# A fused spectral filter and gated MLP on one core: contiguous blocks for the channel products, a held load queue and one zero product less

## The chip, the cores and the metric

The kernel runs on one core of one Trainium2 chip. The metric is the device time of one execution in microseconds. The kernel before was timed three times: 181.11 us is the median, and the runs lie between 180.49 and 181.13 us. One more execution was recorded by the profiler. It took 181.27 us, of which 179.5 us are the span from the first to the last instruction of the program, and every instruction time below comes from it.

## The reference

```python
def reference(A_x, A_w_r, A_w_i, B_x, B_w_gate, B_w_up, B_w_down):
    ...
    x = A_x                                    # (1, 2048, 512) bf16
    xn = _layernorm(x, axis=-1)
    return x + _A_ref(xn, A_w_r, A_w_i) + _B_ref(xn, B_w_gate, B_w_up, B_w_down)
```

`_A_ref` is a two-dimensional real FFT over 2048 tokens and 512 channels, a product with the complex weight `w_r + i w_i` (2048 x 257), and the inverse FFT. `_B_ref` is a gated MLP: `(gelu(xn @ w_gate) * (xn @ w_up)) @ w_down` with an inner width of 1792. Both see the same normalised `xn`, and `B_x` is not used.

## The kernel before, in words

**Stages.** The 2048 tokens are 16 blocks of 128 (`s`), in four groups of four blocks (`b`). For each block VectorE takes the statistics (`stats`, L496 and L497) and normalises (`norm`, L513); TensorE transposes by a product with an identity matrix (`turn`, L526), and VectorE copies the result to `xnT` (L531). The MLP works on `xnT`: `first` (L669) makes the first three of 14 chunks of the inner width for the first two blocks alone, in products of 128 columns, `gated` (L650) all others, in products of 256 and then 512 columns, with gelu and copy on ScalarE (L655, L656) and the product of both on VectorE (L657); `down` (L695) multiplies by `w_down`.

**The spectral half.** For each group `fold` (L537) adds and subtracts mirrored channels on VectorE and then makes two *channel products* (`f_c`, L555 to L566): eight matmuls each, L563, into two PSUM banks of a tile `ps_sp`, from the folded tokens `z` and the small cosine and sine tables `Tf`. Four of the eight have 128 columns (frequencies 0 and 2 modulo 4), four have 256 (odd frequencies). ScalarE then copies the 1024 columns of the tile into `Y` (L569), with the frequencies in order. Token transforms (L776), the weight product on VectorE, inverse token transforms (L851, L852) and inverse channel products (L916) follow.

In PSUM a bank of 512 columns is seen as `(s r i)`: two halves `s` (cosine, sine), two rows `r` (even, odd), 128 columns `i`. The 128-column products share the even row: one writes its columns 0, 2, 4, ..., the other 1, 3, 5, .... The 256-column products write the odd rows as two runs of 128 neighbours:

```python
bank = spb(t, o).rearrange("p (s r i) -> p s r i", s=2, r=2)
even = bank[:, :, 0].rearrange("p s (i h) -> p s i h", h=2)
...
    to = even[:, :, :, cc] if cc < 2 else bank[:, :, 1]
    mat = Tf.ap[:, cc] if cc < 2 else Tf.ap[:, 2 * cc - 2:2 * cc]
    ins = e.matmul(to, z.ap[:, j, o, cc * P:(cc + 1) * P], mat, start=(cc == 0), stop=(cc == 3))
```

**Order of the work.** Every operation is noted with an engine, an estimated cost and a key. A planner (`_Sched.run`, L184) then goes through a model of the five engines and one DMA pipe and fixes for each engine the order in which it issues; `emit` (L249) writes that order out with semaphore waits. TensorE takes up spectral work as soon as the model has it ready, and MLP products, in a fixed order (`fkey`), otherwise. The planner's cost of a channel product is `4 * 0.057 + 4 * 0.11`, 0.67 us.

**Loads.** SyncE (SP) issues nearly all DMAs, in this order: four loads of 128 KB with blocks 0 to 3 of `x`; `wg` and `wu` columns 384 to 768; blocks 4 to 7 of `x`; `wg` and `wu` columns 768 to 1280 and 1280 to 1792; the rest of `small` (the tables `Tf`, `Ti`); blocks 8 to 15 of `x`; `wd`, `tokf`, `toki`; the mirrored copies of the spectral weight, and the weight itself. ScalarE's queue issues three loads at the start: the identity (part 0 of `small`, 32 KB), and columns 0 to 384 of `wg` and `wu` (384 KB each). No load waits for anything but its own data.

**The start.** Before data arrives TensorE runs products on a tile of zeros (`warm`, L483, 128x512): ten with key -50 (`WARM`), and two more with key -30 that the planner puts right behind them. Then come the transposes of block 0, `first` on block 0, the transposes of block 1 and so on.

Of the kernel before, what the change touches and what calls it, by code (L numbers as in the profile page):

```python
# [7 lines left out]
ACT = mybir.ActivationFunctionType  # L8
# [7 lines left out]
P = 128  # L16
NFC = 14
NHALF = 6
NFIRST = 3
WARM = 10  # L20
HKEY = 1.5
NORM = 14.0, 1.5
STAT = 13.0, 1.6
# [12 lines left out]
def _constants():  # L36
    npbf = mybir.dt.np(BF16)
    th = 2.0 * np.pi / S
    m = np.arange(P)
    K = np.zeros((8, P))  # L40
    K[0] = 8 * (2 * (m % 64) + m // 64)
    for v, c in enumerate((4, 1, 9, 2, 10, 3, 11)):
        K[v + 1] = c + 16 * m
    q = np.arange(P) + 0.5
    ph = th * q[:, None, None] * K[None]
    co, si = np.cos(ph), np.sin(ph)
    si2 = si.copy()
    si2[:, 0, 0] = np.sin(th * q * 1024)
    cof = co.copy()
    cof[:, 0, 0] *= 0.5  # L50
    tf = np.stack([cof, si2, -si2], 1)
    ci, sv = co[:64].transpose(2, 1, 0), si2[:64].transpose(2, 1, 0)
    sg = np.array([0, 1, 1, 1, 1, -1, -1, -1])[:, None]
    pr = np.concatenate([ci, -sg * sv], 2)
    pi = np.concatenate([sv, sg * ci], 2)
    lo = (m < 64)[:, None]
    for a in (pr, pi):
        half = a[:, 0, 0:64].copy()
        a[:, 0] = np.concatenate([half * lo, half * ~lo], 1)
    ti = np.stack([pr, pi, -pi], 2)  # L60
    a = 2.0 * np.pi / D * (np.arange(P) + 0.5)[:, None]
    ke = 2 * np.arange(P)[None]
    kse = ke.copy()
    kse[0, 0] = 256
    T = np.stack([np.cos(a * ke), np.cos(a * (ke + 1)), np.sin(a * kse), np.sin(a * (ke + 1))], 1)
    al = np.full((P, 4), 2.0)
    al[0, 0] = al[0, 2] = 1.0
    Ti = T.transpose(2, 1, 0) * al[:, :, None] / (S * D)
    fwd = []
    for d0, r, n in ((0, 0, 64), (0, 2, 64), (0, 1, P), (P, 1, P)):  # L70
        kk = np.arange(r, 256, 4 if n == 64 else 2)[None]
        ks = np.where(kk == 0, 256, kk)
        a = 2.0 * np.pi / D * (d0 + np.arange(P) + 0.5)[:, None]
        fwd += [np.cos(a * kk), np.sin(a * ks)]
    small = np.concatenate([np.eye(P)] + fwd + [Ti.reshape(P, 512)], 1)

    def cvt(z):
        return np.ascontiguousarray(z.reshape(P, -1).astype(np.float32).astype(npbf))

    return cvt(small), cvt(tf), cvt(ti)  # L80
# [47 lines left out]
class _Sched:  # L128
# [11 lines left out]
    def op(self, eng, cost, fn, reads=(), writes=(), tiles=(), key=0.0, after=(), dma=0, lag=0.0, due=None):  # L140
        o = _Op()
        o.eng, o.fn, o.cost, o.key, o.dma, o.lag, o.due = eng, fn, cost, key, dma, lag, due
        o.reads, o.writes, o.tiles = reads, writes, [(t, False) for t in tiles]
        o.extra = [a for a in after if a is not None]
        o.seq = len(self.ops)
        o.end = None
        o.pos = None
        self.ops.append(o)
        return o
# [182 lines left out]
def bass_parallel_sum__spectral_gfnet__glu_gated_geglu__prompt_kernel(  # L332
# [11 lines left out]
    c_small = nc.inline_tensor(small_np, name="c_small")  # L344
# [9 lines left out]
    sch = _Sched()  # L354
    op = sch.op

    with ExitStack() as es:
        def sb(name, shape, dt=BF16, cell=0):
            n = int(np.prod(shape))
            t = es.enter_context(nc.sbuf_tensor(name, [P, n], dt))  # L360
            return view(t, name, 0, shape, cell)
# [18 lines left out]
        small = sb("smallc", [11, P])  # L380
# [22 lines left out]
        ident = small[:, 0]  # L403
# [18 lines left out]
        def spb(t, h, lo=0, n=512):  # L422
            b = (2 * t.slot + h) * 512 + lo
            return ps_sp[:, b:b + n]

        def spair(t):
            return ps_sp[:, t.slot * 1024:(t.slot + 1) * 1024]
# [10 lines left out]
        def c_act(n):  # L438
            return 0.17 + n * 0.000833

        def dma(q, dst, src, nbytes, wr=None, rd=None, key=0.0, after=(), cost=0.41, lag=0.0):
            return op(q, cost, lambda e: e.dma_start(dst() if callable(dst) else dst.ap, src() if callable(src) else src.ap),  # L442
                      reads=rd if rd is not None else (), writes=wr if wr is not None else (), dma=nbytes, key=key, after=after, lag=lag)

        def tt(o, a, b, f, n, key=0.0, **kw):
            return op("dve", c_tt(n), lambda e: e.tensor_tensor(o.ap, a.ap, b.ap, f), reads=(a, b), writes=(o,), key=key, **kw)  # L446
# [4 lines left out]
        def load(q, dst, src, nbytes, **kw):  # L451
            return dma(q, dst, lambda: src, nbytes, wr=(dst,), **kw)

        def blk(s):
            return (s - 1) % 16

        def wload(q, dst, src, lo, hi, **kw):
            load(q, dst[:, :, lo:hi], src[:, :, lo:hi], (hi - lo) * 1024, **kw)

        k = iter(np.arange(0.0, 1.0, 0.001))  # L460
        for s in range(4):
            load("sp", x[:, s], xb[:, blk(s), :], 131072, key=next(k))
        load("act", ident, c_small.ap()[:, 0:P], 32768, key=-9)
        wload("act", wg, wgv, 0, 384, key=0.5)
        wload("act", wu, wuv, 0, 384, key=0.5)
        for w, v in ((wg, wgv), (wu, wuv)):
# [2 lines left out]
        for lo, hi in ((768, 1280), (1280, FF)):  # L469
            for w, v in ((wg, wgv), (wu, wuv)):  # L470
                wload("sp", w, v, lo, hi, key=next(k))
        load("sp", small[:, 1:11].rs([10 * P]), c_small.ap()[:, P:], 327680, key=next(k))
        for b in (2, 3):
            load("sp", x[:, 4 * b:4 * b + 4], xb[:, 4 * b - 1:4 * b + 3, :], 524288, key=next(k))
        op("pool", 0.1, lambda e: e.memset(eps.ap, LN_EPS), writes=(eps,), key=-2)
# [6 lines left out]
        def warm(key):  # L482
            op("pe", 0.38, lambda e: e.matmul(ps_dn[:, :], zero.ap[:, 0:P], zero.ap, start=True, stop=True), reads=(zero,), tiles=(wt,), key=key)  # L483

        for _ in range(WARM):
            warm(-50)


        def xs(s):
            return x[:, s]  # L490
# [4 lines left out]
        def stats(s, key, due=None, after=()):  # L495
            op("dve", 0.63, lambda e: e.bn_stats(bst[:, s].ap, xs(s).ap), reads=(xs(s),), writes=(bst[:, s],), key=key, due=due, after=after)  # L496
            op("dve", 0.172, lambda e: e.bn_aggr(bag[:, s].ap, bst[:, s].ap), reads=(bst[:, s],), writes=(bag[:, s],), key=key, due=due)  # L497
# [36 lines left out]
        Y = R1(0, [8, 2, D])  # L534
        H = R3(0, [8, 2, D])
        X = R1(0, [8, 2, D])
        def fold(b):  # L537
            par = b % 2
            a = RB(2048 * par, [4, 2, P])
            f = RB(4096 + 2048 * par, [4, 4, P])  # L540
            z = R3(2048 * par, [2, 2, 512])
            xt = xnT[:, b]
            kk = 2.0
            tt(a, xt[:, :, 0:2], xt[:, :, 2:4], ADD, 1024, kk)
            tt(f[:, :, 0], a[:, :, 0], a[:, :, 1], ADD, 512, kk)
            tt(f[:, :, 1], a[:, :, 0], a[:, :, 1], SUB, 512, kk)
            tt(f[:, :, 2:4], xt[:, :, 0:2], xt[:, :, 2:4], SUB, 1024, kk)
            fv = f.rs([2, 2, 4, P])
            zv = z.rs([2, 2, 4, P])
            tt(zv[:, :, 0], fv[:, :, 1], fv[:, :, 0, :, ::-1], ADD, 1024, kk)  # L550
            tt(zv[:, :, 1], fv[:, :, 1], fv[:, :, 0, :, ::-1], SUB, 1024, kk)
            for j in range(2):
                t = _T("sp")

                def f_c(e, z=z, j=j, t=t):  # L555
                    ins = None
                    for o in range(2):
                        bank = spb(t, o).rearrange("p (s r i) -> p s r i", s=2, r=2)
                        even = bank[:, :, 0].rearrange("p s (i h) -> p s i h", h=2)
                        for cc in range(4):  # L560
                            to = even[:, :, :, cc] if cc < 2 else bank[:, :, 1]
                            mat = Tf.ap[:, cc] if cc < 2 else Tf.ap[:, 2 * cc - 2:2 * cc]
                            ins = e.matmul(to, z.ap[:, j, o, cc * P:(cc + 1) * P], mat, start=(cc == 0), stop=(cc == 3))  # L563
                    return ins

                op("pe", 4 * 0.057 + 4 * 0.11, f_c, reads=(z[:, j], Tf), tiles=(t,), key=kk, lag=0.1)  # L566
                jp = 2 * b + j
                yv = Y[:, jp].rs([4, P, 2])
                op("act", c_act(1024), lambda e, yv=yv, t=t: e.activation(yv.ap, spair(t).rearrange("p (s r i) -> p s i r", s=4, r=2), ACT.Copy),  # L569
                   writes=(yv,), tiles=(t,), key=-0.5)  # L570

        stats(0, -60.0)
        stats(1, -55.0, None, (sch.ops[-1],))
        root_act(0, 1, -60.0)
        op("act", 1.5, lambda e: e.activation(tmp.ap, eps.ap, ACT.Gelu_apprx_tanh), reads=(eps, rs[:, 0:1]), writes=(tmp,), key=-30.0)
# [9 lines left out]
        for s in (2, 3):  # L585
            norm(s, -50.0)
            turn(s, 1, -50.0)
        fold(0)
        for s in range(4, 16):
            stats(s, 0.0, STAT[0] + STAT[1] * (s - 4))  # L590
# [170 lines left out]
        for v in range(8):  # L761
            c = v // 2
            t = _T("sp")
# [75 lines left out]
        for v in range(8):  # L839
            t = _T("sp")  # L840
# [61 lines left out]
        for jq in range(4):  # L902
# [6 lines left out]
            for jp in (2 * jq, 2 * jq + 1):  # L909
                t = _T("sp")  # L910
# [57 lines left out]
```

## Time and profile before

| what | value |
|---|---|
| median of three runs | 181.11 us |
| the profiled execution | 181.27 us, span 179.5 us |
| TensorE (PE) busy | 173.8 us, 97% of the span |
| VectorE (DVE) busy | 137.6 us, 77% |
| ScalarE (ACT) busy | 108.0 us, 60% |
| channel products L563 | 64 matmuls, 3.9% of the span in the chain that ended last |
| copies of their tiles L569 | 8, 1022 ns each |
| DMA, first quarter of the span | mostly 330 to 367 GB/s |

Busy times count an engine's instructions, not its waits. The profile ends a matmul by a model, so that two matmuls in a row overlap in it; what a matmul costs TensorE is read from the distance between starts, or from the chain that ended last, which gives each piece the time that it added. A `q` behind an engine's name is its sequencer, which issues DMAs. A load is listed with the time from its issue to its landing.

### The profile page before, as it was taken

The numbers are of one execution on the slowest core, as the hardware profiler recorded it, in microseconds if no ns is written. First come the engines' busy times: TensorE is split into PE (matmuls) and PEld (weight loads), VectorE is DVE, ScalarE is ACT, GpSimd is POOL, SyncE is SP. The second block draws the span as 40 slices with busy tenths as digits, with TensorE's granted clock in tenths as the row PEclk, the third lists the DMA queues.
The fourth block names the chain that finished last, engine by engine and source line by source line (L and its number), as shares of the span: only waits on it lengthen the run. The fifth ranks groups of instructions, "written<-read, shape, count | busy, mean of one in ns | idle before, by whom it ended". The sixth has DMA issues, their size and how long they took to land.

```text
span 179.5 us, 2752 instructions
## 1 busy us (share of the span) xinstructions
PE 173.8 (97%) x1042; PEld 93.2 (52%) x1054; DVE 137.6 (77%) x269; ACT 108.0 (60%) x173; POOL 8.0 (4%) x19
## 2 busy tenths in 40 slices
PE   7699999999999999999999999999999999999994
PEld 2398555645466644444444464464444466544443
DVE  2479699987754799429999949949999935995931
ACT  3368766665385865896655386695746389873000
POOL 3120202300000000000000000000000000000000
PEclk9999999999999999999999999999999999999999
DMA  5999997222563600000000000000000000330311
GB/s 153 330 347 358 349 367 265 59 60 52 108 148 76 174 0 0 4 0 0 0 0 0 4 2 0 0 4 0 0 0 0 5 0 0 102 106 29 117 58 60
DMA packets 17773, 14.97 MB, mean 83 GB/s; under 512 B 1247, under 2 KB 17376, under 8 KB 17760
## 3 DMA queue, kind: packets, MB, share of 16 engines
q1 hardware_dynamic: 16560, 13.98, 26.1%
q10 hardware_dynamic: 1200, 0.82, 1.5%
q8 instruction: 8, 0.13, 0.3%
q14 instruction: 5, 0.04, 0.1%
HBM read 12.70 MB, written 3.15 MB: 88 GB/s over the span
## 4 chain that ended last, share of the span: by engine, by line
PE 94%; DMA 4%; ACTq 1%; issue 0%; DVE 0%
PE ps_gu L650 52%; PE ps_dn L695 20%; PE ps_sp L695 7%; PE ps_sp L563 4%; DMA wu<-in_B_w_up_dram 4%; PE ps_sp L776 3%; PE ps_sp L916 2%; PE ps_sp L526 2%; PE ps_sp L851 1%; PE ps_sp L852 1%; PE ps_gu L669 1%; ACTq L442 1%; PE ps_dn L669 0%; DVE x_sb L706 0%
## 5 line engine op out<-in xcount | busy, mean ns | idle before, releaser
L650 PE MATMUL ps_gu<-xnT,wg 128*128 128x512 bf16 (+1 forms) x236 | 56.7, 363 | 0.0
L650 PE MATMUL ps_gu<-xnT,wu 128*128 128x512 bf16 (+1 forms) x236 | 56.7, 363 | 0.0
L656 ACT ACTIVATE uu<-ps_gu 128x512 bf16<-128x512 f32 (+1 forms) x59 | 33.8, 572 | 12.8 <-PE ps_gu L650 12.4
L655 ACT ACTIVATE gg<-ps_gu 128x512 bf16<-128x512 f32 (+1 forms) x59 | 33.8, 572 | 12.4 <-PE ps_gu L650 11.1
L695 PE MATMUL ps_dn<-wd,hT 128*128 128x512 bf16 x158 | 37.2, 379 | 0.5
L650 PEld LDWEIGHTS ps_gu<-xnT,wu 128*128 128x128 bf16 x236 | 22.9, 98 | 22.4
L650 PEld LDWEIGHTS ps_gu<-xnT,wg 128*128 128x128 bf16 x236 | 22.6, 98 | 20.9
L657 DVE TENSOR_TENSOR hT<-gg,uu 128x512 bf16<-128x512 bf16 (+1 forms) x59 | 22.9, 399 | 13.6 <-ACT uu L656 13.5
L695 PEld LDWEIGHTS ps_dn<-wd,hT 128*128 128x128 bf16 x168 | 16.4, 98 | 19.1
L446 DVE TENSOR_TENSOR specB<-specB 128x1024 bf16<-128x1024 bf16 (+2 forms) x37 | 23.5, 673 | 0.6 <-ACT specB L921 0.5
L703 ACT ACTIVATE db<-ps_dn 128x512 bf16<-128x512 f32 x12 | 7.2, 597 | 19.7 <-PE ps_dn L695 19.7
L496 DVE BATCH_NORM_STATS2 bst<-x_sb 128x6 f32<-128x512 bf16 x16 | 11.0, 685 | 4.9 <-DMA x_sb<-in_A_x_dram 4.8
L446 DVE TENSOR_TENSOR specB<-specA 128x2048 bf16<-128x2048 bf16 x8 | 9.4, 1222 | 5.3 <-ACT specA L569 3.9
L695 PE MATMUL ps_sp<-wd,hT 128*128 128x512 bf16 (+2 forms) x69 | 12.2, 336 | 0.1
L446 DVE TENSOR_TENSOR specC<-specB 128x1024 bf16<-128x1024 bf16 (+1 forms) x14 | 10.0, 765 | 0.0
L781 ACT ACTIVATE specA<-ps_sp 128x1024 bf16<-128x1024 f32 x8 | 8.1, 1046 | 2.5 <-PE ps_sp L776 2.5
L569 ACT ACTIVATE specA<-ps_sp 128x1024 bf16<-128x1024 f32 x8 | 7.9, 1022 | 2.8 <-PE ps_sp L563 2.8
L695 PEld LDWEIGHTS ps_sp<-wd,hT 128*128 128x128 bf16 x70 | 6.4, 98 | 6.1 <-DVE x_sb L706 0.2
L446 DVE TENSOR_TENSOR specB<-specB,filt 128x2048 bf16<-128x2048 bf16 x8 | 9.4, 1215 | 0.0
L921 ACT ACTIVATE specB<-ps_sp 128x1024 bf16<-128x1024 f32 x8 | 8.3, 1057 | 0.1
L857 ACT ACTIVATE specC<-ps_sp 128x1024 bf16<-128x1024 f32 x8 | 7.9, 1032 | 0.1
L563 PE MATMUL ps_sp<-smallc,specC 128*128 128x128 bf16 (+1 forms) x64 | 7.8, 293 | 0.0
(64 smaller groups left out, 143.1 us busy)
## 6 DMA issues: line engine op xcount, KB each, us to landing
out_dram<-x_sb SPq DMA_DIRECT2D x15, 128.0 KB, 1.8
wd<-in_B_w_down_dram SPq DMA_DIRECT2D x1, 1792.0 KB, 13.3
x_sb<-in_A_x_dram SPq DMA_DIRECT2D x3, 512.0 KB, 8.5
wg<-in_B_w_gate_dram SPq DMA_DIRECT2D x2, 512.0 KB, 8.9
wu<-in_B_w_up_dram SPq DMA_DIRECT2D x2, 512.0 KB, 9.0
filt<-w_mirror SPq DMA_DIRECT2D x6, 128.5 KB, 2.4
tokf<-c_tf SPq DMA_DIRECT2D x1, 768.0 KB, 13.7
toki<-c_ti SPq DMA_DIRECT2D x1, 768.0 KB, 9.7
```

Source lines behind the costliest of these rows:

```text
L446: return op("dve", c_tt(n), lambda e: e.tensor_tensor(o.ap, a.ap, b.ap, f), reads=(a, b), writes=(o,), key=key, **kw)
L496: op("dve", 0.63, lambda e: e.bn_stats(bst[:, s].ap, xs(s).ap), reads=(xs(s),), writes=(bst[:, s],), key=key, due=due, after=after)
L563: ins = e.matmul(to, z.ap[:, j, o, cc * P:(cc + 1) * P], mat, start=(cc == 0), stop=(cc == 3))
L569: op("act", c_act(1024), lambda e, yv=yv, t=t: e.activation(yv.ap, spair(t).rearrange("p (s r i) -> p s i r", s=4, r=2), ACT.Copy), writes ...
L650: ins = e.matmul(gub(t, n), w.ap[:, dc, fc * P:(fc + 1) * P], xnT.ap[:, b, sl, dc, :], start=(dc == 0), stop=(dc == 3))
L655: op("act", c_act(n), lambda e: e.activation(gg.ap[:, gs.slot, 0:n], gub(g, n), ACT.Gelu_apprx_tanh), tiles=(g, gs), key=0.0)
L656: op("act", c_act(n), lambda e: e.activation(uu.ap[:, us.slot, 0:n], gub(u, n), ACT.Copy), tiles=(u, us), key=0.0)
L657: op("dve", c_tt(n), lambda e: e.tensor_tensor(hT.ap[:, h.slot, lo:lo + n], gg.ap[:, gs.slot, 0:n], uu.ap[:, us.slot, 0:n], MUL), tiles=(g ...
L695: ins = e.matmul(bank(), hT.ap[:, hs[(b, fc)].slot, sl * P:(sl + 1) * P], wd.ap[:, fc, lo:lo + n], start=(fc == 0), stop=(fc == NFC - 1))
L781: fwd.append(op("act", c_act(1024), lambda e, xv=xv, t=t: e.activation(xv.ap, spair(t), ACT.Copy), writes=(xv,), tiles=(t,), key=-0.5))
L857: op("act", c_act(1024), lambda e, gv=gv, t=t: e.activation(gv.ap, spair(t).rearrange("p (k x i) -> p k x i", k=4, x=4), ACT.Copy), writes ...
L921: op("act", c_act(1024), lambda e, rv=rv, t=t: e.activation(rv.ap, spair(t), ACT.Copy), writes=(rv,), tiles=(t,), key=-0.5)
```

## The change

Three edits.

- The bank of a channel product is now seen as two halves `s`, four rows `r` and 64 columns `i`, row `r` holding the frequencies that are `r` modulo 4. A 128-column product writes row 0 or 2 of both halves, that is two runs of 64 neighbours. A 256-column product writes rows 1 and 3 of both halves, four runs of 64; its table is ordered to match (frequencies 1 modulo 4, then 3 modulo 4). ScalarE's copy reads four rows in turn where it read two, and writes `Y` as before.
- Every load on SP's queue from the fifth on waits for the statistics of block 0 (`stats(0)`, the L497 that writes `bag`). The three loads of ScalarE's queue don't wait. The load of the identity takes the first 128 columns of the tables along: 64 KB in rows of 512 B, where it was 32 KB in rows of 256 B; the later load of the tables is 32 KB smaller.
- `WARM` is 9, so that eleven products on zeros are run where there were twelve.

The planner's costs are not changed, but it plans with the new waits.

```diff
-WARM = 10
+WARM = 9
...
-    for d0, r, n in ((0, 0, 64), (0, 2, 64), (0, 1, P), (P, 1, P)):
-        kk = np.arange(r, 256, 4 if n == 64 else 2)[None]
+    for d0, r in ((0, (0,)), (0, (2,)), (0, (1, 3)), (P, (1, 3))):
+        kk = np.concatenate([np.arange(i, 256, 4) for i in r])[None]
...
+        gate = []
+
         def dma(q, dst, src, nbytes, wr=None, rd=None, key=0.0, after=(), cost=0.41, lag=0.0):
+            after = tuple(after) + tuple(gate if q == "sp" else ())
...
-        load("act", ident, c_small.ap()[:, 0:P], 32768, key=-9)
+        load("act", small[:, 0:2].rs([2 * P]), c_small.ap()[:, 0:2 * P], 65536, key=-9)
...
-        load("sp", small[:, 1:11].rs([10 * P]), c_small.ap()[:, P:], 327680, key=next(k))
+        load("sp", small[:, 2:11].rs([9 * P]), c_small.ap()[:, 2 * P:], 294912, key=next(k))
...
-                        bank = spb(t, o).rearrange("p (s r i) -> p s r i", s=2, r=2)
-                        even = bank[:, :, 0].rearrange("p s (i h) -> p s i h", h=2)
+                        bank = spb(t, o).rearrange("p (s r i) -> p s r i", s=2, r=4)
                         for cc in range(4):
-                            to = even[:, :, :, cc] if cc < 2 else bank[:, :, 1]
+                            to = bank[:, :, 2 * cc] if cc < 2 else bank[:, :, 1::2]
...
-                yv = Y[:, jp].rs([4, P, 2])
-                op("act", c_act(1024), lambda e, yv=yv, t=t: e.activation(yv.ap, spair(t).rearrange("p (s r i) -> p s i r", s=4, r=2), ACT.Copy),
+                yv = Y[:, jp].rs([4, 64, 4])
+                op("act", c_act(1024), lambda e, yv=yv, t=t: e.activation(yv.ap, spair(t).rearrange("p (s r i) -> p s i r", s=4, r=4), ACT.Copy),
...
         stats(0, -60.0)
+        gate.append(sch.ops[-1])
+        for o in [o for o in sch.ops if o.eng == "sp"][4:]:
+            o.extra.append(gate[0])
```

## The prediction

> **What bounds the kernel now.** I read the page first: the shares of the engines, the 40 slices, and the chain that ended last.
>
> ```profile
> span 179.5 us, 2752 instructions
> ...
> PE 173.8 (97%) x1042; PEld 93.2 (52%) x1054; DVE 137.6 (77%) x269; ACT 108.0 (60%) x173; POOL 8.0 (4%) x19
> ...
> PE   7699999999999999999999999999999999999994
> ```
>
> TensorE has work in every slice but the first, part of the second and the last. The chain that ended last puts 94% of the span on PE. So a microsecond less of TensorE work, or TensorE running dense a microsecond earlier, is a microsecond off the end, as long as VectorE's spectral chain keeps up. Two places matter for the change: the start, and the channel products. The start, in the timeline (start, length, engine, line):
>
> ```profile
> 1.33 4.91 PE L483 MATMUL ps_dn<-zero 128*128 128x512 bf16 x12 [1.33 <-POOL mhalf L476]
> ...
> 6.08 0.39 PE L526 MATMUL ps_sp<-smallc,specB 128*128 128x128 bf16 x4
> ...
> 6.98 0.40 PE L669 MATMUL ps_gu<-xnT,wg 128*128 128x128 bf16 x4 [0.52 <-DVE xnT L531]
> ...
> 8.32 0.40 PE L669 MATMUL ps_gu<-xnT,wu 128*128 128x128 bf16 x4 [0.94 <-DMA wu<-in_B_w_up_dram]
> ```
>
> After the twelve zero products TensorE waits for `xnT` of block 0, does one group of four matmuls at 6.98, and then waits for the first columns of `wu` until 8.32. From there it runs nearly without a gap to the end. Why `wu` is late is in the DMA issues (KB each, us from issue to landing):
>
> ```profile
> x_sb<-in_A_x_dram SPq DMA_DIRECT2D x4, 128.0 KB, 4.0
> ...
> wg<-in_B_w_gate_dram ACTq DMA_DIRECT2D x1, 384.0 KB, 4.3
> wu<-in_B_w_up_dram ACTq DMA_DIRECT2D x1, 384.0 KB, 6.6
> wg<-in_B_w_gate_dram SPq DMA_DIRECT2D x1, 384.0 KB, 6.9
> wu<-in_B_w_up_dram SPq DMA_DIRECT2D x1, 384.0 KB, 7.6
> ```
>
> By the issue records and landings, `x` blocks 0 to 3 land at 3.20, 3.91, 6.90 and 7.61, the first `wg` at 5.42, the first `wu` (issued 1.68) at 8.27, the held-to-be `wg` and `wu` (issued 2.59 and 3.06) at 9.45 and 10.64. The channel products, in the chain in order of time (start, time it added):
>
> ```profile
> 11.17 0.87 PE ps_gu L650 x8
> ...
> 29.97 0.87 PE ps_sp L563 x8
> ...
> 145.07 0.89 PE ps_sp L916 x16
> ```
>
> At 11.17 eight matmuls of 256 columns take 0.87, 0.109 each. At 145.07 sixteen of 128 columns, into neighbouring columns, take 0.89, 0.056 each. L563 has four of each kind, and its eight take 0.87 as well. So with 0.109 for each of the wide ones, (0.87 - 0.436) / 4 = 0.109 is left for each narrow one: writing every second column they cost as much as matmuls twice their width.
>
> **Part one, the blocks.** The nearest rows for the new narrow write are L851 and L852 (128 columns as two runs of 64): in the chain each adds 0.06, their starts lie 0.056 apart. The new wide write is four runs of 64; no row shows that, the bounds are 0.109 (256 columns in long runs) and twice that, if a short run cost what a stepped column costs. I take 0.109, since L851 shows that runs of 64 cost nothing extra. A channel product then takes 4 x 0.056 + 4 x 0.109 = 0.66, 0.21 less. Eight of them: **1.70 us** off TensorE, all on the path. At the bad bound of the wide writes the edit would lose 8 x 0.22 = 1.8. ScalarE's copy L569 reads single elements in steps already; it takes 1022 ns where straight reads (L781) take 1046. Bounds for the new order: 0.03 less or more, eight times, beside TensorE and on an engine with 40% idle. Nothing.
>
> Does the gain last? The next engine is VectorE. Where a TensorE instruction of the spectral half waits for VectorE, I took the end of its last producer: the token transforms start 1.89 behind it (67.72 against 65.82), the inverse ones over 3, the transposes at 24.60 1.90 behind. VectorE itself idles for TensorE's results before each stage (3.30 at 59.07 before the token stage, 2.63 at 107.66, 3.30 at 149.47), so its chains move forward with the products. What doesn't move are the loads.
>
> **Part two, the held loads.** The wait sits in front of the fifth load on SP. Behind it in that queue stand all other loads; no compute is issued there. The statistics that release it end at 4.13, so the fifth load goes out at about 4.2 where it went out at 2.59, the sixth at 4.65 (3.06), `x` 4 to 7 at 5.1 (3.62). From 4.39 on SP's issues are themselves held up by full queues (1.3 and 2.4 us for one), so by the second part of `wu` (5.73 to 8.12) the queue has caught up. Those who wait: L650 at 11.01 and 11.45 for `wg` and `wu` (landed 1.56 and 0.80 before), L496 at 12.75 for `x` 4 to 7 (0.58 before), L496 at 20.90 for `x` 8 to 11 (no reserve on VectorE, but 1.90 until the transposes need it).
>
> What it may bring: in 3.5 to 6 us the engines move 130 to 165 KB per half microsecond, about full rate, yet `x` 2 and 3 and `wu` finish two microseconds after the 1.3 MB ahead of them could be through (1.34 MB at 350 GB/s is 3.8 us, from 2.2 on: 6.0). Some engines lag, with packets of up to 1.3 us, while others already work on the fifth load. With the queue empty behind `x` 3, I take it that `wu` lands before 6.9. Bounds: no earlier at all, and 6.0.
>
> **Part three, eleven zero products.** Matmuls on zeros start 0.43 apart up to 5.57, the twelfth at 5.86, the transposes 0.22 later at 6.08. The normalised block 0 is ready at 5.38, so the transposes move to 5.86: 0.22, worth something only when `wu` is no longer the later wait. Planner and identity load: 32 KB more at 350 GB/s is 0.09 us of transfer before data needed 2.8 us after it landed (3.03); in the plan it shifts the first loads alike. I give reordering 0.3 us either way.
>
> **The sum.** With `wu` there, the transposes at 5.86 put the group of `wg` at 6.76 (0.90 later, as now) and that of `wu` at 6.98, against 8.32: 1.34 earlier. Then the next need binds: the products at 11.45 need the sixth load. If it still lands at 10.64, they start at 10.69, 0.76 earlier; if it lands with the rest, 1.34. I take the middle, 1.05. 1.70 + 1.05 = 2.75 off the profiled 181.27 is 178.5. That execution lies 0.16 above the median, so the forecast for the median is **178.4**. At 24.60 the reserve to `x` 8 to 11 shrinks from 1.90 to 0.85, still not the bound.
>
> **The rivals.**
> *The hold frees nothing (0.24).* The first `wu` lands at 8.27 as before. For it: the fifth load's first packets run at 5.9, and in the records the last three engines to finish `wu` run at full rate then; they were late already, at 3.4 to 4.7. Against: their stalls fall into the time when SP's issues pile up. Time: 181.1 - 1.7 = 179.4. The Trainium skill ("DMA: Bandwidth & Descriptors", section on queues, rings and completion order) has each DMA engine alternate between its queue rows and keep order within one, so loads behind `x` 3 in SP's row couldn't have delayed `x` 2 and 3; by that rule, on which the long packets speak neither way, this rival would hold.
> *The blocks are no faster (0.07).* The change would not do what it says if the price lay in the change of rows and not in the step. L851 speaks against it. Time: 181.1 - 1.05 = 180.1.
> *More at the start (0.08).* All early loads land together by 9: 1.34 for the start, the 0.2 wait at 11.97 gone, and planner luck of 0.3: 181.1 - 1.7 - 1.34 - 0.5 = 177.5.
> *The TensorE clock stays low (0.11, the slower side).* Zero products start 0.43 apart up to 5.57, then 0.22: full speed came at about 5.7, 4.4 us after the first. Now TensorE's first unbroken run ends at about 6.1, and a pause to 6.8 follows. If full speed then comes only after as long a run again, from 6.8 to about 11.5, the 56 small matmuls of L669 and L526 take 0.107 for 0.056 (2.9) and eight of 256 columns 0.216 for 0.109 (0.86): 178.4 + 3.7 = 182.1. It turns the result to slower when the low clock lasts past about 11. Against: one run of 4.4 us still fits before the pause. The Trainium skill ("TensorE: Matmul & The Clock Gate", Part 1, what's actually happening) has the clock opened by one busy window of 3.4 us that runs free of the program; by that estimate one window lost costs half of it, 1.7 us, 180.1, and 4.4 us in this trace agrees with a window and a part.
>
> **How the numbers follow.** 178.4 has 0.50. A measurement of this kernel tells about 0.5%, 0.9 us, from no change. Faster than 180.2: 0.50 + 0.22 (hold frees nothing, without bad luck) + 0.03 + 0.08 = 0.83. Within: 0.02 + 0.04 + 0.02 = 0.08. Slower: 0.09. The range runs from the good case, 177.5, to 180.2, which takes in the hold without effect and the blocks without most of theirs.
>
> **What would show it.** L563 in the chain at 0.66 for eight; starts 0.056 and 0.109 apart. The wait of L669 for `wu` gone or under 0.3, and its landing before 7; `wg` 384 to 768 issued at 4.2. Zero products: the tenth or eleventh already under 0.43. The prediction is wrong if the wide products take over 0.109, if a wait for `wu`, for `x` 8 to 11 or at 67 to 80 us takes the gain back, or if small matmuls run 0.107 apart after 6.8.

## The result and the profile after

The changed kernel takes 178.81 us (median of four runs, 178.46 to 178.96), the kernel before in the same comparison 180.90. The ratio is 0.9884 with a 95% interval of 0.9858 to 0.9910, so 1.6 to 2.6 us less. The profiled execution took 178.78 us with a span of 177.0, 2.5 below that of the kernel before. Line numbers have moved by three to five: L486 are the products on zeros, L529 the transposes, L674 the products of `first`, L565 the channel products. First the page:

```profile
span 177.0 us, 2763 instructions
...
PE 172.9 (98%) x1053; PEld 91.5 (52%) x1053; DVE 137.6 (78%) x269; ACT 107.9 (61%) x173; POOL 8.0 (5%) x19
...
PE   6899999999999999999999999999999999999994
```

TensorE is still the bound. It is filled from the third slice on, as before; the second slice has risen from 7 tenths to 8. The timeline at the start (start, length, engine, line):

```profile
1.33 4.88 PE L486 MATMUL ps_dn<-zero 128*128 128x512 bf16 x11 [1.33 <-POOL mhalf L479]
...
6.00 0.63 PE L529 MATMUL ps_sp<-smallc,specB 128*128 128x128 bf16 x4
...
7.15 0.40 PE L674 MATMUL ps_gu<-xnT,wg 128*128 128x128 bf16 x4 [0.52 <-DVE xnT L534]
...
7.54 0.40 PE L674 MATMUL ps_gu<-xnT,wu 128*128 128x128 bf16 x4
```

The timeline marks no wait for `wu` where it marked 0.94 (the starts leave 0.16 of it), and the first group on `wu` starts at 7.54 where it started at 8.32. But the transposes take 0.63 for 0.39: their starts lie 0.107 apart, the clock is still low. The DMA issues (KB each, us to landing):

```profile
wg<-in_B_w_gate_dram ACTq DMA_DIRECT2D x1, 384.0 KB, 4.0
wu<-in_B_w_up_dram ACTq DMA_DIRECT2D x1, 384.0 KB, 5.8
```

`wu` lands at 7.50, 0.77 earlier. The chain in order of time (start, time it added):

```profile
10.40 0.87 PE ps_gu L655 x8
...
29.20 0.66 PE ps_sp L565 x8
```

The eight matmuls of a channel product (L565) add 0.66 where they added 0.87; eight matmuls of 256 columns in long runs add 0.87 as before. All of the difference lies in these two places. The span from the first group on `wu` to the end is 171.16 us before and 169.46 after: 1.70 less, which is taken for the blocks until the experiments below separate the edits. The rest, 0.77, is the earlier first group.

### The profile page after: what moved, and what is told of

Its sections match the earlier page's. It is cut to its first block, busy times and chain, and to the rows that moved or that the text cites. A ratio compares the mean times of both kernels' runs of the same rounds, so it can differ in the third digit from the quotient of the medians.

```text
span 177.0 us, 2763 instructions
## 1 busy us (share of the span) xinstructions
PE 172.9 (98%) x1053; PEld 91.5 (52%) x1053; DVE 137.6 (78%) x269; ACT 107.9 (61%) x173; POOL 8.0 (5%) x19
## 4 chain that ended last, share of the span: by engine, by line
PE 98%; DVE 0%; POOL 0%; issue 0%; POOLq 0%
PE ps_gu L655 53%; PE ps_dn L700 20%; PE ps_sp L700 7%; PE ps_sp L781 3%; PE ps_sp L565 3%; PE ps_dn L486 3%; PE ps_sp L529 2%; PE ps_sp L921 2%; PE ps_gu L674 1%; PE ps_sp L856 1%; PE ps_sp L857 1%; PE ps_dn L674 1%; POOL zero L480 0%; DVE xnT L534 0%; DVE x_sb L711 0%
## 5 line engine op out<-in xcount | busy, mean ns | idle before, releaser
L700 PE MATMUL ps_dn<-wd,hT 128*128 128x512 bf16 x168 | 39.0, 379 | 0.0
L571 ACT ACTIVATE specA<-ps_sp 128x1024 bf16<-128x1024 f32 x8 | 7.9, 1021 | 1.8 <-PE ps_sp L565 1.6
L449 DVE TENSOR_TENSOR specA<-specB 128x2048 bf16<-128x2048 bf16 (+1 forms) x8 | 7.5, 979 | 0.0
```

The source lines that it names most:

```text
L700: ins = e.matmul(bank(), hT.ap[:, hs[(b, fc)].slot, sl * P:(sl + 1) * P], wd.ap[:, fc, lo:lo + n], start=(fc == 0), stop=(fc == NFC - 1))
```

## The experiments

The theory to be tested after the result: the blocks give 1.70, the hold gives 0.77. The rival: the hold gives nothing, and the landing of `wu` differs from execution to execution. I read the same three numbers from every profile: when the first `wu` lands, when the first group on it starts, and the span from there to the end. The medians of the kernel before lie between 180.62 and 180.90 in the comparisons.

| kernel | `wu` lands | first group | to the end | median | ratio, 95% interval |
|---|---|---|---|---|---|
| before | 8.27 | 8.32 | 171.16 | 180.90 | |
| changed | 7.50 | 7.54 | 169.46 | 178.81 | 0.9884 (0.9858 to 0.9910) |
| blocks alone | 7.42 | 7.75 | 169.44 | 179.18 | 0.9914 (0.9889 to 0.9939) |
| hold alone | 7.32 | 7.52 | 171.16 | 180.51 | 0.9998 (0.9984 to 1.0013) |
| zeros alone | 7.26 | 7.31 | 171.16 | 180.57 | 1.0015 (0.9988 to 1.0042) |
| changed without hold | 7.53 | 7.58 | 169.47 | 178.85 | 0.9904 (0.9883 to 0.9925) |
| before, again | 8.27 | 8.31 | 171.15 | 180.87 | 1.0000 (0.9979 to 1.0021) |
| wide products stepped | 7.60 | 7.64 | 172.87 | 182.29 | 1.0088 (1.0075 to 1.0101) |
| changed, seven zeros | 7.43 | 7.48 | 169.45 | 179.01 | 0.9921 (0.9892 to 0.9950) |
| changed, four zeros | 7.53 | 7.57 | 171.84 | 180.74 | 0.9982 (0.9959 to 1.0006) |
| hold at the third load | 6.23 | 6.84 | 169.73 | 178.73 | 0.9887 (0.9873 to 0.9901) |
| hold to the landing of `x` 0 | 6.44 | 6.63 | 170.04 | 178.73 | 0.9882 (0.9865 to 0.9899) |
| weights ahead of `x` 2, 3 | 8.54 | 8.59 | 169.81 | 180.21 | 0.9962 (0.9948 to 0.9975) |
| next weights cut | 6.48 | 6.72 | 171.29 | 179.62 | 0.9939 (0.9917 to 0.9961) |

### Each edit alone

**Blocks alone**: the kernel before with the first edit's lines of the diff above and nothing else.

> The kernel before with the blocks of 64 columns alone. Theory: the blocks bring 0.21 us for each of eight channel products and all of it reaches the end, so 1.70 us below the kernel before (about 179.2), with eight products in 0.66 us in the chain; TensorE waits for the first wu until about 8.3 us as before. Rival (the wu of the changed kernel landed early by chance and not by the hold): wu lands at about 7.5 here too, and the time is 2.4 us below.

**Hold alone**: the lines of `gate` and of the identity load.

> The kernel before with the held loads and the wider identity load alone. Theory: wu lands at about 7.5 and not 8.3, the first group on wu starts 0.8 us earlier, and this reaches the end: 0.8 us below the kernel before, about 180.1. Rival (the hold frees nothing): wu at 8.2 or later and the same time as before within 0.2 us.

**Zeros alone**:

```diff
-WARM = 10
+WARM = 9
```

> The kernel before with nine products on zeros in place of ten. Theory: the wait for wu stands behind the transposes, so nothing moves: within 0.15 us of the kernel before. Rival (fewer products on zeros put off full clock): the transposes start about 6.0 but run 0.107 us apart, and if the small products after 6.8 do too, 2 us or more above the kernel before.

**Changed without hold**: the changed kernel without the lines of `gate`.

> The changed kernel without the hold: blocks, nine products on zeros, wider identity load. Theory: the start is that of the kernel before, wu at about 8.3, so 1.7 us below the kernel before (179.2), and 0.8 above the changed kernel. Rival (the start was gained by the other two edits or by chance): 2.5 us below, as the changed kernel.

The span from the first group on is 171.16 with the old products and 169.44 to 169.47 with the blocks, whichever of the other edits is in. So the first half of the theory stands to 0.02 us. The second half is not borne out. Hold alone is not faster: by its interval 0.29 us less at best, 0.23 more at worst. The wider identity load, which is in it as well, was not tried by itself. And three profiles without any hold have `wu` at 7.26 to 7.53. The expectation of 0.8 for the hold is missed, and so is that of a late `wu` wherever the hold is left out. The timelines of the blocks alone and of the hold alone:

```profile
6.42 0.58 PE L526 MATMUL ps_sp<-smallc,specB 128*128 128x128 bf16 x4
7.52 0.40 PE L668 MATMUL ps_gu<-xnT,wg 128*128 128x128 bf16 x4 [0.52 <-DVE xnT L531]
7.75 0.39 PE L668 MATMUL ps_gu<-xnT,wu 128*128 128x128 bf16 x4
```

```profile
7.28 0.40 PE L675 MATMUL ps_gu<-xnT,wg 128*128 128x128 bf16 x4 [0.52 <-DVE xnT L534]
7.52 0.39 PE L675 MATMUL ps_gu<-xnT,wu 128*128 128x128 bf16 x4
```

In neither does TensorE wait for `wu`: the transposes come late behind slow zeros, `xnT` with them, and `wu` has landed 0.33 and 0.20 before its group starts. Where the clock opens late, an earlier `wu` has nothing to give.

### A second look at the kernel before

> The kernel before once more, for a second look at its start. Theory now: the landing of the first wu at 8.27 was the late end of a spread that has nothing to do with the later loads; in this profile it lands between 7.2 and 7.7, as in five other profiles with and without the hold, and the time is that of the kernel before. Rival (the hold does help and the other profiles were lucky): wu at 8 or later again.

Missed too: `wu` landed at 8.27 again. The timeline of this run:

```profile
6.34 0.40 PE L669 MATMUL ps_gu<-xnT,wg 128*128 128x128 bf16 x4 [0.52 <-DVE xnT L531]
8.31 0.40 PE L669 MATMUL ps_gu<-xnT,wu 128*128 128x128 bf16 x4 [1.57 <-DMA wu<-in_B_w_up_dram]
```

The clock opened earlier here, `xnT` was ready 0.64 earlier, and the wait for `wu` took all of it: 181.26 us and a span of 179.5 again. Both profiled executions of the kernel before lie at the slow end of its runs (180.07 to 181.40 in the first comparison of experiments); a start at 7.5 makes about 180.5. In the packet records both have single packets of over 1 us on SP's queue between 4.2 and 4.7 us (1.33; 1.02 and 1.38), and no other profile shows one between 2 and 6 us. So there is a late landing, seen in two of six profiles without the hold and in none of four with the hold at the fifth load. Whether the hold removes it was not settled: two of six could be chance, and the times bound the gain at 0.3 us.

### What the first `wu` waits for

**Hold at the third load**, and **hold to the landing of `x` 0**. In the changed kernel:

```diff
-        for o in [o for o in sch.ops if o.eng == "sp"][4:]:
+        for o in [o for o in sch.ops if o.eng == "sp"][2:]:
```

and, for the second of the two, also

```diff
-        gate.append(sch.ops[-1])
+        gate.append(sch.ops[0])
```

> The changed kernel with the hold two loads earlier: blocks 2 and 3 of x wait as well, so that until 4.3 only blocks 0 and 1 of x, the identity, wg and wu are in flight. Theory (wu is paced by the transfers that are really in flight beside it): 256 KB fewer beside it, 0.7 us, wu lands at about 6.8; then the transposes at 6.0 are the later wait, the first group on wu starts at about 7.3, 0.2 earlier than in the changed kernel, and the time is at most 0.3 us below it, unless blocks 2 and 3 of x come too late for the statistics at 7.3 and 8.7. Rival (landing is set by stalls of single DMA engines): wu at 7.3 to 7.5 as before and the same time.

> As the changed kernel, but SP waits from its third load on for the landing of block 0 of x (3.3 us) and not from its fifth for the statistics of it (4.25). Theory: blocks 2 and 3 of x come behind most of wu, as in the kernel with the hold at the third load, so wu lands at about 6.4; all later loads go out 0.9 earlier than there, so that the second part of wu lands at about 9.5 and not 10.2 and doesn't stop TensorE at 10; 0.5 to 0.7 us below the changed kernel, about 178.2. Rival (the early start puts blocks 2 and 3 of x beside wu again): wu at 7.3 and the time of the changed kernel.

**Weights ahead of `x` 2 and 3**: blocks alone, with the fifth and sixth load issued as third and fourth.

```diff
-        for s in range(4):
+        for s in range(2):
             load("sp", x[:, s], xb[:, blk(s), :], 131072, key=next(k))
...
             wload("sp", w, v, 384, 768, key=next(k))
+        for s in range(2, 4):
+            load("sp", x[:, s], xb[:, blk(s), :], 131072, key=next(k))
```

> The kernel with the blocks alone and no hold, but with the fifth and sixth loads of SP (wg and wu, columns 384 to 768) issued ahead of blocks 2 and 3 of x. Theory (SP's row is served in order, so a later load delays what stands behind it in the row and takes its share beside the other row): the first wu lands at about 8 or later, since 768 KB and not 256 KB now run beside it, blocks 2 and 3 of x land after 8.5, and the time is up to 1 us above the kernel with the blocks alone. Rival (the order on SP does not matter to wu): wu at 7.3 to 7.6.

The timeline of the last of the three:

```profile
8.59 0.62 PE L670 MATMUL ps_gu<-xnT,wu 128*128 128x128 bf16 x8 [0.17 <-DMA wu<-in_B_w_up_dram]
```

The three agree with each other. With 256 KB fewer in flight beside it, `wu` lands at 6.23 and 6.44. With the weights in front of `x` 2 and 3 it lands at 8.54, and `x` 2 and 3 at 9.47 and 9.84. So what stands in front in SP's queue counts for `wu` in the other queue. The Trainium skill ("DMA: Bandwidth & Descriptors", queues, rings and completion order) has each DMA engine alternate between the queues that have work for it and take each in order. This trace agrees: the loads of SP's queue land in the order of issue in every run.

The packet records also show why the hold at the fifth load changes so little. The first packets of the fifth load (768 bytes; those of `x` have 1024) start at 5.89 in the kernel before, where that load is issued at 2.59, and at 5.94 in the changed kernel, where it is issued at 4.28. In all ten profiles in which `x` 0 to 3 are issued at once they start between 5.89 and 6.02, held or not, while `wu` is still under way. A hold that ends at 4.2 is over long before that. What these packets cost `wu` from 5.9 on was not tested.

But the gain of 0.7 to 0.9 at the first group ends 2.5 us later. The timelines of the two kernels with an early `wu`:

```profile
6.84 0.39 PE L674 MATMUL ps_gu<-xnT,wu 128*128 128x128 bf16 x4
...
10.34 0.60 PE L655 MATMUL ps_gu<-xnT,wu 128*128 128x256 bf16 x4 [0.23 <-DMA wu<-in_B_w_up_dram]
```

```profile
6.63 0.39 PE L674 MATMUL ps_gu<-xnT,wu 128*128 128x128 bf16 x4
...
10.44 0.60 PE L655 MATMUL ps_gu<-xnT,wu 128*128 128x256 bf16 x4 [0.53 <-DMA wu<-in_B_w_up_dram]
```

The columns 384 to 768 of `wu` land at 10.21 and 10.30, as in the changed kernel (10.29), since the same bytes stand before them. Products that start at 10.67 in the changed kernel start at 10.34 and 10.44: 0.2 to 0.3 is left, and the medians, 178.73, can't be told from 178.81. The expected 178.2 is missed.

**Next weights cut**, to shorten those bytes, on top of the hold to `x` 0:

```diff
-            wload("sp", w, v, 384, 768, key=next(k))
+            wload("sp", w, v, 384, 640, key=next(k))
...
-        for lo, hi in ((768, 1280), (1280, FF)):
+        for lo, hi in ((640, 1152), (1152, FF)):
```

> As the kernel with the hold at the third load until block 0 of x lands, with the next loads of wg and wu cut to columns 384 to 640 (256 KB each), then 640 to 1152 and 1152 to 1792. Theory (the start is now bound by the bytes ahead of the second wu): 256 KB fewer stand before that wu lands, 0.75 us at 350 GB/s, so it lands at about 9.6 and the wait of 0.53 before the products at 10.44 is gone; 0.5 us below that kernel and the changed one, 178.2. Rival (rows of 512 B for these loads, or the later x, cost as much): the same 178.7.

```profile
12.99 1.03 PE L655 MATMUL ps_gu<-xnT,wg 128*128 128x256 bf16 x8 [0.96 <-DMA wg<-in_B_w_gate_dram]
14.39 1.05 PE L655 MATMUL ps_gu<-xnT,wu 128*128 128x256 bf16 x8 [0.37 <-DMA wu<-in_B_w_up_dram]
```

The wait at 10.4 is gone (`wu` at 9.72), and 0.9 us slower than its base all the same: columns 640 to 768 now come with the next load, behind `x` 4 to 7, and TensorE waits 0.96 and 0.37 for them. I had cut the load and not looked at who needs the rest.

### The step in the channel products

**Wide products stepped**: the kernel before, in which the narrow products write runs of 64 and the wide ones every second column. The table of transforms and ScalarE's copy are those of the first edit, so that the odd frequencies reach `Y` in another order and the output is not that of the reference; shapes and counts stay. Only the core is shown.

```diff
-    bank = spb(t, o).rearrange("p (s r i) -> p s r i", s=2, r=2)
-    even = bank[:, :, 0].rearrange("p s (i h) -> p s i h", h=2)
+    bank = spb(t, o).rearrange("p (s c) -> p s c", s=2)
+    odd = bank[:, :, 128:256].rearrange("p s (i r) -> p s r i", r=2)
...
-    to = even[:, :, :, cc] if cc < 2 else bank[:, :, 1]
+    to = bank[:, :, 64 * cc:64 * cc + 64] if cc < 2 else odd
```

> The kernel before with narrow products in blocks of 64 neighbours and the 256-column products on every second column. The frequencies reach Y in another order, so the output is another; all shapes and counts stay. Theory: a stepped column costs two, whatever the width: the wide product takes 0.216 for 0.109, eight products of a channel product 4 x 0.056 + 4 x 0.216 = 1.09 against 0.87, so 8 x 0.22 = 1.8 us above the kernel before. Rival (the price lay in two products sharing one row of the bank, not in the step): 0.66 for eight and 1.7 below.

```profile
29.29 1.09 PE ps_sp L563 x8
```

The eight matmuls of a channel product add 1.09, as the step theory says. The span from the first group to the end grows from 171.16 to 172.87, which is 1.71 above the kernel before and 3.41 above the blocks: 32 wide products at 0.107 each. Here no two products share a row of the bank, so the rival, the shared row, is out.

### Products on zeros and the clock

**Seven and four zeros**: the changed kernel with `WARM = 7` and `WARM = 4`, which is nine and six products on zeros in all, since two more are issued apart from these.

> The changed kernel with seven products on zeros in place of nine (nine with the two of the other key). Theory: the transposes are ready at about 5.55 and start there, 0.45 earlier, at half clock; the first wu is the later wait, so at most 0.2 us is gained; if TensorE has too little work before full clock, some executions are 2 us longer. Rival (zeros do not matter for the clock): no execution stands out.

> The changed kernel with four products on zeros in place of nine (six with the two of the other key). Theory (full clock needs a long run of TensorE work first): TensorE is idle from about 3.9 to 5.55, so many executions reach full clock only after 8 us; the 60 small products until the wide ones then run 0.107 us apart, and the median is 1 to 3 us above the changed kernel, with a wide spread. Rival (full clock comes a fixed time after the first product, with or without a pause): the median of the changed kernel, 178.8, within 0.3.

With four (six in all) the last product on zeros starts at 3.44 and the transposes at 5.56, and the timeline shows the low clock lasting:

```profile
7.97 0.63 PE L529 MATMUL ps_sp<-smallc,specB 128*128 128x128 bf16 x4
8.40 0.63 PE L674 MATMUL ps_gu<-xnT,wg 128*128 128x128 bf16 x4
```

Groups of four stay 0.43 apart up to 12.67 and the span to the end is 2.4 longer; the median is 1.9 above the changed kernel. With seven the median is the same, but two of seven runs took 180.07 and 180.40 where the other five lie between 178.43 and 179.19. With nine alone two of twelve runs took 182.41 and 182.57, the others at most 181.16. None of these four was profiled. The record gives a mean granted clock of 0.99 for three of them and 1.0 for the run of 180.07; it also gives 1.0 for the profiled run with four, although its small products ran 0.107 apart up to 12.67, so this figure does not count a clock that is low from the start. That all of them are one effect is therefore not shown. Nor do such runs come with fewer zeros alone: one run of the kernel before, with twelve, took 182.73 at a granted clock of 0.991.

## Why the prediction was right, and where it was not

- **The blocks, 1.70**: right, and to 0.01: 0.66 for eight, starts 0.056 and 0.109 apart, 171.16 to 169.46. Its price of 0.109 for a narrow stepped product is a mean: the starts before lay 0.067, 0.110, 0.150 and 0.110 apart, so that part of the cost shows only at the products behind. The bound at which runs of 64 cost double for the wide products did not come; the step alone costs, at either width. The copy L571 takes 1021 ns, as L569 did.
- **The start, 1.05**: the size was wrong, and the cause not borne out. The step that failed is "with the queue empty behind `x` 3, I take it that `wu` lands before 6.9". It landed at 7.50, among the landings of four of the six profiles without a hold (7.26 to 7.60), and the hold alone gains 0.3 us at most. The queue behind `x` 3 was not empty: the fifth load's packets run from 5.9 on, with the hold as without it. The sum under that step was short as well: it took 350 GB/s, where the kernel before moved 287 from 2 to 6 us and the changed one 309, and in the changed kernel 0.50 pass from the end of the last packet of ScalarE's queue (7.00) to the landing. Behind that stands the larger mistake: the wait of one profiled execution, with the group on `wu` at 8.32, was priced as that of all runs, while the three runs known then, 180.49 to 181.13, all lay below its 181.27. The rival "the hold frees nothing" is nearer to what the runs show, but not in its condition, `wu` at 8.27 as before. Its price, 179.4, started from the median of three runs, 181.11, where the later comparisons have 180.62 to 180.90. The changed kernel's 178.81 is what 180.6 to 180.9 and 1.70 give, to 0.4. That the forecast of 178.4 came within 0.4 of it is partly luck: of the 2.75 taken off, the experiments show 1.70, and the hold, from which the other 1.05 was to come, does not show it.
- **The zeros, 0.22**: the transposes were put at 5.86; they ran from 6.00 to 6.63, since the clock opened later in this execution. The eleven products on zeros started 0.40 to 0.43 apart to the last, so the tenth and eleventh showed no full clock. `wu` was still the later wait, by 0.16, so the late transposes cost nothing here.
- **The next need**: right in kind. The second part of `wu` landed at 10.29 and the products on it began 0.38 later, so here it did not bind yet; with a still earlier start it did (10.30 and a wait of 0.53).
- **Does the gain last**: right. The token transforms kept 1.68 of 1.89, the transposes of the second group (23.82) 1.56 of 1.90. Two readings beside it were off: VectorE's 3.30 at 149.47 is a wait before a product of the MLP (L657), not before a spectral stage, and of the "0.2 wait at 11.97" 0.11 is the matmul itself.
- **The slower rival**, the clock: the mechanism exists. It shows with six products on zeros, at 2.4 us in the profile where 3.7 were priced, and in no profile with eleven; the two long runs with eleven stay open.

## What to carry to other kernels

Price a matmul by its output's step as well as by its width: look at the distance between starts, and compare with a row of the same width that writes neighbours. Before a wait in one profile is priced, compare that execution with the spread of the runs, and take a second profile if the wait is of the size of the spread. In these runs a load was delayed by what stood in front, in its own queue and the other one, and a hold that ended before the queue would have served the held load changed little. Moving a load forward paid only until the next bytes bound.

## What the runs showed of the hardware

- A matmul of 128 or 256 columns that writes every second column of PSUM takes 0.109 or 0.216 in the mean, about twice 0.056 or 0.109 (0.87 and 1.09 for eight, with 0.66 for runs of neighbours). Runs of 64 neighbours cost nothing extra.
- Full clock came between 2.7 and over 5.4 us after the first product on zeros, which starts at 1.33, with the same products back to back up to there: at about 4.0, 4.4, 5.4, 5.7, 6.3 and after 6.7 in six profiles. The Trainium skill ("TensorE: Matmul & The Clock Gate", Part 1) gives around 4 us with 0.5 either way, for a window of 3.4 us that runs free of the program; the spread here is wider than that figure. With six products on zeros and nothing from there to 5.56 it came at about 12.8.
